# Zero products in the gaps of two attention chains, down blocks begun with the first weight chunk, half of one batch's attention moved under down products

## The chip, the cores and the metric

The kernel runs on one core of one Trainium2 chip. The metric is the time of one execution on the device in microseconds. A run of a kernel is one execution; a *round* runs the kernel before and the changed one on the same chip.

## The reference

```python
# q, k, v: (8, 8, 576, 64), phi: (8, 8, 576, 32)
a = exp(phi - max(phi, axis=2)); a = a / sum(a, axis=2)
k_m = einsum('bhsm,bhsd->bhmd', a, k)          # 32 memory slots a head
v_m = einsum('bhsm,bhsd->bhmd', a, v)
attn = softmax(q @ k_m^T / 8)                  # 576 x 32 a head
x = (attn @ v_m) transposed to (4608, 512)
out = ((x @ w_a) * (x @ w_b)) @ w_out          # 512 -> 1536 -> 512
```

## The kernel before

In what follows PE is the matrix engine (TensorE), ACT is ScalarE, DVE VectorE and POOL GpSimd; PSUM is the memory that PE's results go to. The kernel never forms x. It *folds* v_m into w_a and w_b for each batch (`vab`), so that an *up step* multiplies these with the normalised attention `A`: four matmuls for `pa`, four for `pb`, a cast of `pa` on ACT, a product on DVE that leaves 128 rows of the hidden layer in `ht`. *Down products* then multiply `ht` with `w_out`; twelve of them make one block of 128 tokens (`po`).

```python
def fold(lo, hi, z, ...):          # 8 small matmuls (64x32 tiles), then two casts
    pvas = [banks.tile([P, 512], F32, name="pva") for _ in range(2)]
    ...                            # pva[g] <- kvT, w_a or w_b columns lo:hi
    # vab[g] <- pva[g]: g = 0 on ACT, g = 1 on DVE

def up(b, i):
    for hf in range(2):
        pa = ps_up.tile([P, HALF], F32, name="pa")      # two buffers
        ...                                             # two matmuls, a_sb <- pa on ACT
    yield                                               # a place for something else
    for hf in range(2):
        pb = ps_up.tile([P, HALF], F32, name="pb")      # two buffers
        ...                                             # two matmuls, ht <- a_sb * pb on DVE
    yield
```

The kernel divides PSUM into eight banks: two for `pa`, two for `pb`, and four that everything else takes in rotation, `banks`: sums, transposes, scores, denominators `pD`, normalisations `pR`, folds and the open block `po` of down products. The order of PE's work is written by hand (cuts are marked with dots):

```python
fill(28)                                  # zero products: keep PE busy while loads are on their way
run(0, "exp0 exp1 ks0 kt0")               # batch 0: exponentials, k sums, transposes
fill(2)
run(0, "qt0 qt1 ks1 kt1")
run(0, "sc0 qt2 qt3")                     # q transposes (DVE), scores
fill(4)
run(0, "sc1 vs vt dn vh0a nr0 nr1 nr2 nr3 vh0b")   # v sums, denominators, folds, normalisations
ups(steps(0, 0, 2), named(0, "- vh1a - vh1b"))     # up steps, with folds at places between them
ups(steps(0, 2, 4), named(0, "- va1a - va1b"))
load(2)
ups(steps(0, 4, 8), named(0, "- va2a - va2b"))
ups(steps(0, 8, 12), named(1, "exp0 exp1"))
run(1, "ks0 kt0 ks1 kt1 qt0 qt1 sc0 qt2 qt3")      # batch 1's chain
some(8)                                            # eight down products of batch 0
...
ups(steps(1, 6, 12), named(2, "qt0 exp0 qt1 exp1 - kv0 kv1 - kvt - qt2 sc0 qt3 sc1"), 0)
work.ready = 2 * S // P * NFF
for x in "va0a dn va0b va1a nr0 nr1 va1b nr2 va2a nr3 va2b".split():
    run(2, x)                                      # the stage of folds and products:
    work.advance(2)                                # two down products behind each item
```

From batch 2 on, every up step has down products beside it, at a rate that uses up what is ready.

The softmax here doesn't subtract the row's maximum and nothing guards it: scores larger than these inputs give would overflow.

## Time and profile before

| | before |
|---|---|
| median of 4 runs | 273.26 us (272.68 to 273.96) |
| span of the profiled run | 271.8 us |
| PE busy | 257.4 us, 95% of the span |
| last fold of batch 0 | at 30.27 us |
| first down product | at 42.33 us |
| batch 1's first pa | at 57.96 us |
| batch 2's first pa | at 86.02 us |
| batch 3's first pa | at 112.10 us |

The kernel is bound by PE from 90 us on, so the reader should look for holes before that. The last five rows of the table are landmarks: they are instructions that both kernels have, so the time between two of them can be compared stage by stage. Busy times of the stages, from the windows view (window, length, busy us and count of PE, PEld, DVE, ACT and POOL, granted clock, DMA share, GB/s):

```profile
30.27:57.96 27.69, 24.88 (x334) 12.43 (x333) 15.17 (x35) 10.49 (x25) 6.68 (x9) 0.94 1.20 228
57.96:77.00 19.04, 17.69 (x253) 10.58 (x251) 15.61 (x37) 12.80 (x33) 2.35 (x4) 1.00 1.05 219
77.00:86.02 9.02, 8.62 (x93) 3.12 (x87) 6.59 (x11) 4.53 (x9) 0.62 (x1) 1.00 0.90 162
86.02:112.10 26.08, 26.08 (x322) 14.68 (x321) 19.39 (x44) 15.30 (x39) 2.98 (x4) 1.00 0.63 123
112.10:271.80 159.70, 154.50 (x1565) 85.38 (x1557) 91.83 (x203) 79.95 (x197) 5.95 (x8) 1.00 0.36 77
```

The rows are: batch 1's chain and first down blocks; batch 1's ups; the stage of folds and products; batch 2's ups; the rest. In the first, PE has 2.8 us of holes, and a mean clock of 0.94 over 27.7 us hides 1.7 us more. In the second it has 1.4 us of holes, while its busy time is stretched by waits inside the matmul records. The third has 0.4 us of holes and the fourth none; the 5.2 us of the last lie behind the last matmul, which ends at 266.6 us.

### The profile page before, as it was taken

The numbers are of one execution on the slowest core, as the hardware profiler recorded it, in microseconds if no ns is written. First come the engines' busy times: TensorE is split into PE (matmuls) and PEld (weight loads), VectorE is DVE, ScalarE is ACT, GpSimd is POOL, SyncE is SP. The second block draws the span as 40 slices with busy tenths as digits, with TensorE's granted clock in tenths as the row PEclk, the third lists the DMA queues.
The fourth block names the chain that finished last, engine by engine and source line by source line (L and its number), as shares of the span: only waits on it lengthen the run. The fifth ranks groups of instructions, "written<-read, shape, count | busy, mean of one in ns | idle before, by whom it ended". The sixth has DMA issues, their size and how long they took to land.

```text
span 271.8 us, 7173 instructions
## 1 busy us (share of the span) xinstructions
PE 257.4 (95%) x2898; PEld 138.5 (51%) x2898; DVE 166.7 (61%) x366; ACT 135.3 (50%) x331; POOL 36.5 (13%) x59
## 2 busy tenths in 40 slices
PE   8869978999989999999999999999999999999992
PEld 3435552446624555555555555555555555666540
DVE  7456863459778568855885567855885477443200
ACT  3037742078555565645565465726563555544220
POOL 8943332010310310031001300000000000000000
PEclk9998997999999999999999999999999999999999
DMA  7999999999893597059615891111112111112243
GB/s 156 195 202 204 252 207 230 229 269 256 165 207 77 128 200 142 14 134 188 134 39 166 136 207 39 41 41 38 34 26 62 42 39 41 40 41 57 65 111 77
DMA packets 25858, 33.49 MB, mean 123 GB/s; under 512 B 1889, under 2 KB 20321, under 8 KB 25825
## 3 DMA queue, kind: packets, MB, share of 16 engines
q0 software_dynamic: 19536, 23.01, 47.2%
q1 hardware_dynamic: 6288, 10.03, 14.7%
q8 instruction: 22, 0.36, 0.5%
q14 instruction: 12, 0.09, 0.1%
HBM read 42.47 MB, written 9.44 MB: 191 GB/s over the span
## 4 chain that ended last, share of the span: by engine, by line
PE 92%; DVE 4%; issue 1%; ACT 1%; DVEq 0%; ACTq 0%
PE po L385 35%; PE pa L455 19%; PE pb L464 19%; PE pva L341 6%; PE pw L119 3%; PE pkv L216 3%; PE pscore L296 2%; DVE qT L203 2%; PE pR L327 1%; DVE ht L467 1%; PE pT L245 1%; PE pk L265 1%; PE pT L251 1%; PE pD L315 1%; PE pT L280 0%
## 5 line engine op out<-in xcount | busy, mean ns | idle before, releaser
L385 PE MATMUL po<-wo_sb,ht 128*128 128x512 f16 x432 | 121.0, 383 | 0.2 <-ACT E L305 0.2
L467 DVE TENSOR_TENSOR ht<-a_sb,pb 128x288 f16<-128x288 f16 x192 | 78.0, 446 | 35.2 <-PE pb L464 30.8
L458 ACT CAST a_sb<-pa 128x288 f16<-128x288 f32 x192 | 67.6, 407 | 34.2 <-PE pa L455 32.4
L464 PE MATMUL pb<-A,vab 128*128 128x288 f16 x384 | 64.8, 288 | 0.5
L455 PE MATMUL pa<-A,vab 128*128 128x288 f16 x384 | 64.0, 289 | 0.2 <-ACT a_sb L458 0.2
L385 PEld LDWEIGHTS <-ht 128*128 128x128 f16 x432 | 41.3, 98 | 24.6 <-issue 3.8
L351 ACT CAST vab<-pva 128x512 f16<-128x512 f32 (+1 forms) x54 | 29.5, 555 | 44.5 <-PE pva L341 44.4
L455 PEld LDWEIGHTS <-vab 128*128 128x128 f16 x384 | 33.0, 98 | 24.8 <-issue 11.3
L464 PEld LDWEIGHTS <-vab 128*128 128x128 f16 x384 | 35.5, 98 | 19.4 <-issue 1.9
L353 DVE CAST vab<-pva 128x512 f16<-128x512 f32 x46 | 31.6, 687 | 7.3 <-PE pva L341 6.7
L394 ACT ACTIVATE o_sb<-po 128x512 f32<-128x512 f32 (+1 forms) x36 | 21.6, 604 | 23.2 <-PE po L385 23.2
L305 ACT ACTIVATE E<-pscore,rphi 128x288 f16<-128x288 f32 x32 | 14.3, 497 | 26.5 <-PE pscore L296 26.5
L203 DVE STREAM_TRANSPOSE qT<-q_sb 128x576 f16<-128x576 f16 x32 | 24.1, 764 | 0.0
L330 DVE SCALAR_TENSOR_TENSOR A<-E,rphi,pR 128x288 f16<-128x288 f16 x32 | 15.9, 512 | 8.7 <-PE pR L327 8.7
L341 PEld LDWEIGHTS <-kvT 64*32 64x32 f16 x400 | 5.9, 89 | 19.3 <-issue 18.1
L78 POOL DMA_DIRECT2D phi_sb<-in_phi_dram x7 | 5.3, 755 | 68.3 <-ACT exp_sb L194 50.9
L319 DVE RECIPROCAL rD<-pD 128x144 f16<-128x144 f32 x8 | 8.5, 1057 | 7.8 <-PE pD L315 7.8
L231 DVE CAST kvm<-pkv 128x128 f16<-128x128 f32 (+1 forms) x16 | 4.1, 267 | 13.8 <-PE pkv L216 13.8
L194 ACT ACTIVATE exp_sb<-phi_sb 128x576 f16<-128x576 f32 x16 | 10.9, 695 | 2.6 <-DMA phi_sb<-in_phi_dram 2.6
L119 PE MATMUL pw<-warm 128*128 128x512 f16 x34 | 9.9, 450 | 1.3 <-DVE warm L113 1.3
L341 PE MATMUL pva<-wa_sb,kvT 64*32 64x512 f16 (+1 forms) x200 | 10.3, 378 | 0.5 <-DVE kvT L253 0.4
L296 PE MATMUL pscore<-qT,kvT 32*32 32x288 f16 x256 | 8.0, 295 | 2.7 <-DVE qT L203 2.7
(44 smaller groups left out, 109.6 us busy)
## 6 DMA issues: line engine op xcount, KB each, us to landing
out_dram<-o_sb SPq DMA_DIRECT2D x72, 128.0 KB, 2.4
kv_sb<-in_v_dram POOLq DMA_DIRECT2D x8, 576.0 KB, 9.9
phi_sb<-in_phi_dram POOLq DMA_DIRECT2D x7, 576.0 KB, 5.2
kv_sb<-in_k_dram POOLq DMA_DIRECT2D x7, 576.0 KB, 7.7
q_sb<-in_q_dram POOLq DMA_DIRECT2D x6, 576.0 KB, 9.3
wo_sb<-in_moe_w_out_dram POOLq DMA_DIRECT2D x3, 512.0 KB, 17.2
q_sb<-in_q_dram POOLq DMA_DIRECT2D x4, 288.0 KB, 12.7
wa_sb<-in_moe_w_a_dram POOLq DMA_DIRECT2D x2, 512.0 KB, 13.3
```

Source lines behind the costliest of these rows:

```text
L119: nc.tensor.matmul(pw[:, :cols], warm[:, :P], warm[:, :cols], start=True, stop=True)
L203: nc.vector.transpose(out=t["qT"][:, hp, :], in_=qs[b][:, hp, :])
L330: nc.vector.scalar_tensor_tensor(out=attn[b][:, g, sl], in0=t["E"][:, g, sl], scalar=t["rphi"][:, g:g + 1], in1=pR, op0=ALU.mult, op1=ALU. ...
L341: nc.tensor.matmul(pvas[g][32 * j:32 * j + 32, 0:hi - lo], t["kvT"][64 * r:64 * r + 64, 4 + g, M * j:M * j + M], w_sbs[z][64 * r:64 * r + ...
L351: nc.scalar.copy(out=vabs[b][z][:, g, lo:hi], in_=pvas[g][:, 0:hi - lo])
L353: nc.vector.tensor_copy(out=vabs[b][z][:, g, lo:hi], in_=pvas[g][:, 0:hi - lo])
L385: nc.tensor.matmul(po, hts[pair][:, i, P * c:P * (c + 1)], wo_sb[:, i, :], start=(i == 0), stop=(i == NFF - 1))
L394: nc.scalar.mul(out=o_sb[:, :cut], in_=po[:, :cut], mul=1.0 / (CS * CS))
L455: nc.tensor.matmul(pa, vab[0][:, g, fs], A[:, g, HALF * hf:HALF * (hf + 1)], start=(g == 0), stop=(g == 1))
L458: nc.scalar.copy(out=a_sb, in_=pa)
L464: nc.tensor.matmul(pb, vab[1][:, g, fs], A[:, g, HALF * hf:HALF * (hf + 1)], start=(g == 0), stop=(g == 1))
L467: nc.vector.tensor_tensor(out=ht[:, i, t0:t0 + HALF], in0=a_sbs[hf], in1=pb, op=ALU.mult)
```

## The change

Its intent, in four parts, A to D:

- **A**, the first chain: 28 zero products in front become 16, and others fill the gaps behind each short group, so that PE's clock holds.
- **B**: for batches 0 and 1, `pb` of the odd steps takes one of the four rotating banks.
- **C**, the second chain: k sums of batch 1 go among the last up steps of batch 0, and down products begin in front of the first scores instead of behind them, about when the first third of `w_out` lands.
- **D**: two q transposes and both scores of batch 2 leave batch 1's ups for the stage of folds and products, which grows from 11 to 17 places.

```diff
--- before.py
+++ after.py
@@ -459,7 +459,7 @@
             a_sbs.append(a_sb)
         yield
         for hf in range(2):
-            pb = ps_up.tile([P, HALF], F32, name="pb")
+            pb = banks.tile([P, HALF], F32, "pb") if b < 2 and i % 2 else ps_up.tile([P, HALF], F32, name="pb")
             for g in range(2):
                 nc.tensor.matmul(pb, vab[1][:, g, fs], A[:, g, HALF * hf:HALF * (hf + 1)],
                                  start=(g == 0), stop=(g == 1))
@@ -490,43 +490,56 @@
         for f in named(b, names):
             f()
 
-    fill(28)
-    run(0, "exp0 exp1 ks0 kt0")
-    fill(2)
-    run(0, "qt0 qt1 ks1 kt1")
-    run(0, "sc0 qt2 qt3")
-    fill(4)
-    run(0, "sc1 vs vt dn vh0a nr0 nr1 nr2 nr3 vh0b")
+    fill(16)
+    run(0, "exp0 exp1 ks0")
+    fill(3, 256)
+    run(0, "kt0 qt0 qt1")
+    fill(7)
+    run(0, "sc0 ks1")
+    fill(3, 256)
+    run(0, "kt1 qt2 qt3")
+    fill(5)
+    run(0, "sc1")
+    fill(3)
+    run(0, "vs dn vt")
+    fill(3, 256)
+    run(0, "nr0 nr1 vh0a nr2 nr3 vh0b")
+    fill(4, 256)
     ups(steps(0, 0, 2), named(0, "- vh1a - vh1b"))
     ups(steps(0, 2, 4), named(0, "- va1a - va1b"))
     load(2)
     ups(steps(0, 4, 8), named(0, "- va2a - va2b"))
-    ups(steps(0, 8, 12), named(1, "exp0 exp1"))
+    ups(steps(0, 8, 12), named(1, "exp0 exp1 - - - ks0 kt0 ks1"))
     early = early_downs()
 
     def some(n):
         for _ in range(n):
             next(early, None)
 
-    run(1, "ks0 kt0 ks1 kt1 qt0 qt1 sc0 qt2 qt3")
+    run(1, "kt1 qt0 qt1")
+    fill(4)
+    some(8)
+    run(1, "sc0 qt2 qt3")
     some(8)
     run(1, "sc1")
     some(8)
     run(1, "dn")
     some(8)
     run(1, "nr0 nr1 nr2 nr3")
-    some(10)
+    some(8)
     run(1, "vs")
     some(4)
-    run(1, "vt va0a")
+    run(1, "vt")
+    some(2)
+    run(1, "va0a")
     some(2)
     run(1, "va0b")
     some(99)
     load(3)
     ups(steps(1, 0, 6), named(1, "- va1a - va1b - va2a - va2b"), 0)
-    ups(steps(1, 6, 12), named(2, "qt0 exp0 qt1 exp1 - kv0 kv1 - kvt - qt2 sc0 qt3 sc1"), 0)
+    ups(steps(1, 6, 12), named(2, "- exp0 qt0 exp1 qt1 - kv0 - kv1 - kvt"), 0)
     work.ready = 2 * S // P * NFF
-    for x in "va0a dn va0b va1a nr0 nr1 va1b nr2 va2a nr3 va2b".split():
+    for x in "qt2 sc0 qt3 sc1 va0a va0b dn va1a va1b nr0 va2a nr1 va2b nr2 - nr3 -".split():
         run(2, x)
         work.advance(2)
     every = "qt0 exp0 qt1 exp1 qt2 kv0 kv1 - kvt sc0 qt3 sc1 - va0a dn va0b nr0 va1a nr1 va1b nr2 va2a nr3 va2b"
```

## The prediction

> **What bounds the kernel now.** I read the page's slices first, then two-microsecond windows of the first 100 us, then the timeline there, and last the landing time of each transfer. The slices:
>
> ```profile
> PE   8869978999989999999999999999999999999992
> PEclk9998997999999999999999999999999999999999
> DMA  7999999999893597059615891111112111112243
> ```
>
> From slice 13 on (about 90 us) PE has no holes until the drain of the last products. The matmul time of that part stays the same in the changed kernel, so all that can be won lies before 90 us: in PE's holes and in slices at a lower clock. The windows show two places:
>
> ```profile
> 18.00:20.00 2.00, 1.29 (x17) 0.94 (x11) 1.55 (x3) 0.65 (x2) 1.00 (x2) 0.77 1.35 204
> 20.00:22.00 2.00, 1.94 (x14) 1.01 (x13) 1.09 (x3) 1.16 (x4) 0.71 (x1) 0.50 1.24 207
> ...
> 38.00:40.00 2.00, 1.34 (x77) 0.88 (x68) 1.22 (x6) 0.00 (x0) 0.74 (x1) 1.00 1.24 207
> 40.00:42.00 2.00, 0.55 (x18) 0.17 (x19) 1.72 (x4) 0.00 (x0) 0.75 (x1) 1.00 1.24 206
> 42.00:44.00 2.00, 2.00 (x20) 0.83 (x20) 1.23 (x2) 0.89 (x2) 0.74 (x1) 0.75 1.24 209
> 44.00:46.00 2.00, 2.00 (x21) 0.42 (x19) 0.00 (x0) 0.04 (x1) 0.00 (x0) 0.50 1.22 207
> 46.00:48.00 2.00, 2.00 (x12) 0.70 (x14) 0.00 (x0) 0.85 (x2) 0.00 (x0) 0.90 1.14 322
> ```
>
> The columns are window, length, busy time of PE, PEld, DVE, ACT, POOL, then the clock, the DMA share and GB/s. PE is busy 1.89 of 4 us in 38 to 42 (batch 1's attention chain), and right after that the clock is halved; the same follows the thin stretch 16 to 20 of batch 0's chain. The last two columns matter as much: DMA runs at some 207 GB/s without a break. It is a bound of its own up to 82 us, and once PE already waits for it:
>
> ```profile
> 30.26 0.11 PEld L341 LDWEIGHTS <-kvT 64*32 64x32 f16 x8 [0.26 <-DMA wb_sb<-in_moe_w_b_dram]
> ```
>
> That is the last fold of batch 0, which needs the last quarter block of w_b, issued at 14.80 with 15.4 us to landing, so in place at 30.2. The third stretch is batch 1's up step, 58 to 77.65:
>
> ```profile
> 58.00:64.65 6.65, 6.65 (x73) 3.91 (x72) 5.52 (x12) 5.52 (x14) 0.00 (x0) 1.00 1.16 271
> ...
> 66.90:77.65 10.75, 9.16 (x175) 5.29 (x173) 8.25 (x22) 6.17 (x17) 2.97 (x4) 1.00 0.96 180
> 77.65:86.18 8.53, 8.37 (x80) 3.05 (x80) 6.61 (x11) 4.13 (x8) 0.00 (x0) 1.00 0.86 155
> ```
>
> Here no products stand beside the ups, and DVE paces PE: in 60 to 70 it is busy 9.48 of 10 us.
>
> **What the Trainium skill says.** "TensorE: Matmul & The Clock Gate", Part 1 (The HAM clock gate): the clock is halved after an idle window of about 3.4 us and comes back after a busy one; K is binary. The trace agrees: time at half speed is 2 x (1 - clock) x 2 us a window, 1.0 + 2.0 + 0.4 = 3.4 us for the second dip; the first adds up to 3.4 as well (0.77, 0.50, 0.87). The trace adds that PE need not be quite idle: 47% busy was enough, 69% (12 to 14) was not. Same page, Part 2 (Step-by-step): matmuls stay in program order, only weight loads are pulled ahead; so a fold that waits for weights holds up everything behind it, as at 30.26. "Perfetto Trace Analysis", Roofline: 16 DMA engines move about 435 GB/s for one core. These transfers cast float32 to float16, so 207 GB/s written is 414 read: the queue is full, and no landing time of the weights can move forward.
>
> **The change part by part.** Durations are those of before at full clock: one product 0.22 us (8 in 1.83), one up step 0.98 (8 matmuls; pa 0.49 and pb 0.49 in the chain), one fold 0.34, one half of the k sums 0.64, scores 0.4 a half, pR 0.5, v sums 0.7.
>
> *Batch 0's chain with fills.* The first fill falls from 28 to 16 products, so ks0 can start at k's landing (1.31 + 5.8 = 7.1) instead of 9.53, and the clock should hold. The chain itself still needs v (landed at 14.6) and rD (1.06) and four normalisations (2 us), so I put the first up step at about 19 instead of 20.64, and steps 0 and 1 save perhaps 1.4 us of half clock. Some 3 us early: but the folds stand at fixed places, and their weights land at 22.6, 25.2, 27.7 and 30.2, while before runs those folds at 25.48, 26.90, 28.82 and 30.26. The lead over the weights shrinks to nothing at the last. So PE waits at each of these folds instead, and stands at 30.26 just where it stood: gain 0.
>
> *30.26 to the end of batch 1's k sums.* Steps 6 to 11 took 7.1 us against 5.9 of matmul time. pb in a second set of buffers removes the waits for DVE (0.1 a step), but the exponentials (1.27 us on ACT) still hold up a_sb and with it pa of step 10. ks0, kt0 and ks1 now lie among the last steps. I work it out to ks1 ending at 38.7 instead of 39.6.
>
> *Down blocks early.* kt1 follows at 39.4 to 39.6 (its cast waits for DVE), four fills 0.87 end at 40.5; the first chunk of w_out is there at 22.93 + 17.2 = 40.1, the second at 42.6, the third at 45.2, v at 48.1. Then PE is full: 48 products (10.6), two scores 0.8, pD 0.25, pR 0.5, v sums 0.7, transposes 0.25, two folds 0.7 = 13.8, so the ups of batch 1 start at about 54.4 instead of 57.96. This holds the clock dip (3.4 us at half clock, 1.7 lost) and the holes of 38 to 42.3, less the fills. The products that used to cover the casts of the last fold are used up by now, so the first pb waits about half a microsecond: I count a gain of 3.5 less 0.3, 3.2.
>
> *Batch 1's ups without half of batch 2's attention.* Before: 57.96 to 77.0, 19.0 us. The first six steps are bound by DVE (0.82 of ht and 0.68 of vab a step with a fold) and stay near 7.9. Steps 6 to 11 lose two transposes (1.54 of DVE) and two scores: DVE 6 x 0.82 + 1.54 + 0.88 + 0.56 = 7.9, PE 5.88 + 1.0 + 0.6 = 7.5, so about 8.4 instead of 11.1. Sum 16.3 plus 0.3 of waiting: 16.6. That is 2.4 earlier, of which 0.8 is only matmul time moved: gain 1.6 to 1.7 (PE's lead is now about 5).
>
> *The stage of folds and products.* Before 9.2 us against 8.1 of matmuls. After: 17 places with 34 products (7.5) + six folds 2.0 + pD 0.25 + pR 0.5 + scores 0.8 = 11.1, and I leave the loss to bank waits at 1.0: three banks remain beside the held one in both. Gain 0; the ten further products are taken from the next stage.
>
> *Batch 2's ups.* 36 products before, 26 after. Matmul time there falls by 2.2 to 24.0 us, while DVE keeps its 20. In the second half a step has one fold and one normalisation on DVE: 0.82 + 0.69 + 0.51 = 2.0, against PE's 2.2 less 0.18 = 2.0. DVE becomes level with PE: I take off 0.6.
>
> Sum: 3.2 + 1.65 + 0 - 0.6 = 4.3 us, and 0.4 for bank waits that the spacing of the 17 places may save: 4.7. 273.6 - 4.7 = 268.9.
>
> **The rivals.** *First: the whole of the early gain comes through.* If the folds of batch 0 didn't wait for weights, the 3 us of the first chain would come on top: 265.9. Against it stand the DMA columns at their ceiling and the wait at 30.26. *Second: the holes move.* If the first products wait for the w_out chunk or the first fold steps of batch 1 are held by ACT (four o_sb of 0.55 beside vab and a_sb), some 1.5 us go: 270.5. For it: DMA is full, and w_out's margin by my working is 0.4 us. *Third: DVE eats the moved work.* If DVE, at 83% in batch 2's ups before, paces both halves of that stage with 10 products fewer, it costs up to 2.2 and leaves 270.5 as well. *Fourth: bank shortage.* pb of the odd steps shares four banks with the folds and held sums; a pb that waits for a fold's eviction would bring back 0.5 to 1 us. Against it: banks are taken in rotation. None of these makes the kernel slower than before, as the fills fall from 34 full ones to 35 full and 13 half ones, all in holes but four.
>
> **Range and chances.** Each of the three main terms (3.2, 1.65, 0.6) is good to about 1 us, together about 1.8; the range is 266.6 to 271.2. The limit of 2% is 268.2, a gain of 5.5, a little past my middle: 0.36 for faster, 0.62 for the same, 0.02 for slower.
>
> **What would show it.** Right: clock 1.00 in 18 to 24 and in 42 to 48; new waits of PE for wa_sb and wb_sb at the folds between 22 and 30, with the last of them still at 30.2; the first product at about 40.5, batch 1's first pa at about 54.4; batch 2's ups at about 83, with DVE over 85% busy in them. The early part is wrong if the last fold of batch 0 runs well before 30 (the transfers were not the bound), the middle if the first product comes after 41, the last if PE shows holes or longer steps after 83.

## More of the kernel before

A program on one core has no second die to compare with, so small differences are compared only where the kernels share a chip and the runs of the kernel before.

## The result, and the profile after

The changed kernel took 270.36 us (median of 4 runs, 269.79 to 270.95), the kernel before 273.26 in the same rounds. The ratio is 0.9893 with a 95% interval of 0.9858 to 0.9927: faster by about 1%, the same by the measure of 2%. Ratios here are the mean time of one kernel's runs over that of the other's of the same rounds, so they are not quite the ratio of the medians quoted beside them.

The slices of the page of the changed kernel:

```profile
PE   8979989999999999999999999999999999999992
PEclk9998999999999999999999999999999999999999
DMA  7999999999993595169515971111111111112243
```

(9 stands for 90% or more of a fortieth of the span, on PEclk for the granted clock.) The dip of the clock near 44 us is gone, one near 20 us is still there, and DMA is saturated as long as before. The windows of the second chain, changed kernel:

```profile
38.00:40.00 2.00, 1.67 (x50) 0.94 (x48) 1.37 (x5) 0.70 (x2) 0.74 (x1) 1.00 1.24 208
40.00:42.00 2.00, 2.00 (x17) 0.94 (x18) 1.67 (x5) 0.00 (x0) 0.75 (x1) 1.00 1.25 207
42.00:44.00 2.00, 2.00 (x25) 0.76 (x24) 1.30 (x2) 0.60 (x2) 0.55 (x1) 1.00 1.24 208
44.00:46.00 2.00, 2.00 (x25) 0.75 (x24) 0.00 (x0) 0.69 (x2) 0.19 (x1) 1.00 1.23 211
```

PE is busy 3.67 of 4 us from 38 to 42, where it was busy 1.89 in the kernel before, and the clock stays at 1.00. The last fold of batch 0 in the timeline of the changed kernel (start, length, what it is; in brackets the idle time before it and what ended that):

```profile
30.75 0.11 PEld L341 LDWEIGHTS <-kvT 64*32 64x32 f16 x8 [0.37 <-DMA wb_sb<-in_moe_w_b_dram]
```

It still waits for the last part of `w_b`, and as that part landed half a microsecond later in this profile, it also runs half a microsecond later than before. The stages of the changed kernel, the same rows as shown of before:

```profile
30.75:55.26 24.51, 23.66 (x336) 12.18 (x337) 14.23 (x34) 10.00 (x24) 6.68 (x9) 1.00 1.21 220
55.26:71.70 16.44, 16.28 (x229) 10.28 (x221) 14.15 (x34) 12.29 (x32) 2.23 (x3) 1.00 1.13 264
71.70:85.48 13.78, 13.21 (x132) 4.63 (x130) 9.53 (x17) 6.33 (x12) 0.74 (x1) 1.00 0.87 156
85.48:108.98 23.50, 23.50 (x310) 13.51 (x309) 18.57 (x43) 14.46 (x37) 2.98 (x4) 1.00 0.68 132
108.98:268.70 159.72, 154.50 (x1565) 85.37 (x1557) 91.82 (x203) 79.95 (x197) 5.95 (x8) 1.00 0.36 77
```

| stage | before | predicted | after |
|---|---|---|---|
| to the last fold of batch 0 | 30.27 | 30.26 | 30.75 |
| to batch 1's first pa | 27.69 | 24.1 | 24.51 |
| batch 1's ups | 19.04 | 16.6 | 16.44 |
| folds and products | 9.02 | 12.1 | 13.78 |
| batch 2's ups | 26.08 | 24.6 | 23.50 |
| the rest | 159.70 | unchanged | 159.72 |

The second column is read off the steps of the prediction (54.4 - 30.26, 71.0 - 54.4 and so on). The rest is the same to 0.02 us, so the whole of the difference lies in five numbers. Two of them are off the prediction by more than a microsecond: the stage of folds and products (1.7 too long) and batch 2's ups (1.1 shorter than forecast). With the half microsecond by which the last fold was late, 0.4 in the second row, 0.2 the other way in the third, and the credit of 0.4 that the prediction had added for bank waits, the forecast gain of 4.7 becomes 4.7 - 1.7 + 1.1 - 0.5 - 0.4 + 0.2 - 0.4 = 3.0, the profile's 3.1 but for rounding.

One figure serves all that follows: **from the last fold to the end**, 241.50 us before and 237.91 after (worked out from the times in the traces themselves, as the pages print the end to 0.1 us only). The time up to the last fold changes from execution to execution with the transfers and the clock; the time from it on hardly does in the changed kernel. In c0 it had its last fold at 31.27 and needed 237.90 from there, and e1, e5 and e6, which change only what lies in front, needed 237.90 to 237.91. For the kernel before there is one trace, and its 241.50 contain a dip of the clock.

### The profile page after: what moved, and what is told of

The parts are those of the page before. It is cut to its first block, busy times and chain, and to the rows that moved or that the text cites. A ratio compares the mean times of both kernels' runs of the same rounds, so it can differ in the third digit from the quotient of the medians.

```text
span 268.7 us, 7200 instructions
## 1 busy us (share of the span) xinstructions
PE 258.4 (96%) x2912; PEld 138.9 (52%) x2912; DVE 166.4 (62%) x366; ACT 135.4 (50%) x331; POOL 36.5 (14%) x59
## 4 chain that ended last, share of the span: by engine, by line
PE 84%; DMA 10%; DVE 2%; issue 1%; POOL 1%; ACT 1%; ACTq 0%; DVEq 0%; POOLq 0%
PE po L385 34%; PE pa L455 19%; PE pb L464 17%; DMA wb_sb<-in_moe_w_b_dram 6%; PE pva L341 6%; DMA kv_sb<-in_v_dram 4%; PE pkv L216 2%; PE pscore L296 2%; PE pR L327 1%; PE pT L245 1%; PE pD L315 1%; PE pT L251 1%; POOL q_sb L90 1%; DVE qT L203 1%; DVE ht L467 0%
## 5 line engine op out<-in xcount | busy, mean ns | idle before, releaser
L464 PE MATMUL pb<-A,vab 128*128 128x288 f16 x384 | 63.8, 288 | 0.3
L119 PE MATMUL pw<-warm 128*128 128x512 f16 (+1 forms) x48 | 13.4, 415 | 1.3 <-DVE warm L113 1.3
L341 PE MATMUL pva<-wb_sb,kvT 64*32 64x512 f16 (+1 forms) x200 | 10.6, 382 | 0.1
```

The costliest lines, as they stand in the source:

```text
L341: nc.tensor.matmul(pvas[g][32 * j:32 * j + 32, 0:hi - lo], t["kvT"][64 * r:64 * r + 64, 4 + g, M * j:M * j + M], w_sbs[z][64 * r:64 * r + ...
L464: nc.tensor.matmul(pb, vab[1][:, g, fs], A[:, g, HALF * hf:HALF * (hf + 1)], start=(g == 0), stop=(g == 1))
```

## The experiments

The theory after reading the two traces: (1) the last fold is tied to its transfer, so part A is worth little as long as the transfer is there; (2) part C carries the gain; (3) part D wins in batch 1's ups, and loses it in the stage of folds and products, where a fold must wait for the banks of its predecessors; the prediction's term for that stage was too small by 1.7 us. Rivals are in the expectations. Each kernel was run 6 times, on three chips; medians of the kernel before were 273.83 (e1 to e4), 274.72 (c0, e5 to e7) and 274.06 (e8 to e11).

### The changed kernel again (c0)

> The changed kernel itself, as the measure for the runs beside it. Expected 270.2 to 270.7 us, with the last fold of batch 0 at the landing of the last part of w_b (30.5 to 31.3) wherever the clock held in the first chain, and no more than 0.5 us spread between runs with and without a dip.

Measured: 270.90 us (269.8 to 272.0), ratio 0.9884 [0.9833, 0.9935]. In this profile the clock held through the first chain, and the timeline shows what the theory says is hidden there:

```profile
28.72 0.41 PE L341 MATMUL pva<-wa_sb,kvT 64*32 64x512 f16 x8 [0.65 <-DMA wa_sb<-in_moe_w_a_dram]
...
31.27 0.41 PE L341 MATMUL pva<-wb_sb,kvT 64*32 64x512 f16 x8 [1.06 <-DMA wb_sb<-in_moe_w_b_dram]
```

With the clock at 1.00, PE reaches the last two folds 0.65 and 1.06 us before their weights. The first chain is faster, and the transfer takes the gain back. The expected time (270.2 to 270.7) was missed by 0.2, and so was the expected spread: five runs at a mean clock of 0.994 to 0.997 took 269.8 to 271.2, and one at 0.982 took 272.0.

### The first chain of before in the changed kernel (e1)

```diff
-    fill(16)
-    run(0, "exp0 exp1 ks0")
-    fill(3, 256)
 ...
-    run(0, "nr0 nr1 vh0a nr2 nr3 vh0b")
-    fill(4, 256)
+    fill(28)
+    run(0, "exp0 exp1 ks0 kt0")
+    fill(2)
+    run(0, "qt0 qt1 ks1 kt1")
+    run(0, "sc0 qt2 qt3")
+    fill(4)
+    run(0, "sc1 vs vt dn vh0a nr0 nr1 nr2 nr3 vh0b")
```

> The changed kernel with the first chain of before (28 fills in front, no fills in the small gaps, old order). Theory (the last fold of batch 0 waits for the last part of w_b, which lands at about 30.5 us whatever PE does before): the last fold stays at 30.2 to 30.8 and the time within 0.4 us of the changed kernel's 270.4, although a clock dip of 3.4 us near 20 us should be back. Rival (the fills of the first chain carry part of the gain): the last fold at 31.5 or later and 1 us or more is lost, 271.4 or more.

Measured: 270.87 us (270.26 to 271.95), ratio 0.9881 [0.9837, 0.9925]. From the last fold to the end 237.90, so nothing behind it changed. In the profile the last fold ran at 31.92, a miss for both sides: the dip lasted two windows in place of one (clock 0.50 from 20 to 24 us, 0.65 and 0.64 on either side of that). Runs with a mean clock of 0.992 and 0.994 took 270.67 and 270.26, those at 0.984 to 0.989 took 270.5 to 271.95. Against e2, which has the new chain and is otherwise equal from the last fold on, the median is 0.5 us higher. So part A is worth about half a microsecond by these medians, though the ranges of the runs overlap. That it comes through the clock is likely: between 16 and 28 us the four profiles of the old chain have one dip (before) or two in a row (e1, e6, e8), the ten of the new chain one (six of them) or none (c0, e3, e4, e7).

### The last third of w_b not transferred, with both chains (e5, e6)

The fold reads the middle third of `w_b` a second time. The results are wrong.

```diff
-    load_wab(1024, 1536)
+    nc.gpsimd.dma_start(out=wa_sb[:, :, 1024:1536], in_=wa_rows[:, :, 1024:1536])
 ...
-                        w_sbs[z][64 * r:64 * r + 64, hp, lo:hi],
+                        w_sbs[z][64 * r:64 * r + 64, hp, (lo - 512 if z and lo == 1024 else lo):(hi - 512 if z and lo == 1024 else hi)],
```

> The changed kernel without the transfer of the last third of w_b (0.5 MB); the fold reads the middle third again, so the result is wrong on purpose. Theory (transfers pace batch 0's ups once the clock holds): the wait of about 1 us at the last fold is gone, it runs at 29.8 to 30.3, and the time falls by 0.7 to 1.2 us against the changed kernel of the same rounds. Rival (the wait hides another limit, such as the casts on ACT and VectorE): under 0.3 us.

> The same without the last third of w_b, and with the first chain of before; wrong on purpose too. Theory (the old chain with its dips gets to the last fold just when its weights land, so it cannot use the free transfer): within 0.4 us of the old chain with the transfer (about 0.4 above the changed kernel), and 1.0 to 1.6 us above the new chain without the transfer: that is what the fills would be worth if the weights were there. Rival (the first chain is worth nothing at all): no difference between the two chains here either.

Measured: e5 (new chain) 269.92 us (269.56 to 270.46), e6 (old chain) 271.03 us (269.7 to 271.78); the changed kernel 270.90. Without the transfer the new chain gains 1.0 us, and its last fold runs at 29.87 even with a dip in the profile. The old chain stays at 271.03, with the last fold at 31.42, and gains nothing. The two chains differ by 1.1 us here and by about 0.5 with the transfer. That is the theory's first point: by the medians the fills are worth about a microsecond, and the transfer of `w_b` hides half of it.

### Part C alone in the kernel before (e8)

```diff
-    ups(steps(0, 8, 12), named(1, "exp0 exp1"))
+    ups(steps(0, 8, 12), named(1, "exp0 exp1 - - - ks0 kt0 ks1"))
 ...
-    run(1, "ks0 kt0 ks1 kt1 qt0 qt1 sc0 qt2 qt3")
+    run(1, "kt1 qt0 qt1")
+    fill(4)
+    some(8)
+    run(1, "sc0 qt2 qt3")
 ...
-    some(10)
+    some(8)
 ...
-    run(1, "vt va0a")
+    run(1, "vt")
+    some(2)
+    run(1, "va0a")
```

> The kernel before with the second chain of the change alone (k sums of batch 1 among the last ups, down blocks begun with the first chunk): old first chain, no extra buffers for pb, no move of batch 2's attention. Theory (this part carries nearly all of the gain): from the last fold of batch 0 to the end 238.2 to 238.8 us instead of 241.5, and 2.5 to 3.5 us under the kernel before of the same rounds. Rival (the parts only work together): under 1.5 us.

Measured: 272.58 us (271.0 to 273.58), the kernel before 274.06; ratio 0.9944 [0.9902, 0.9986]. From the last fold to the end 238.88, just outside the expected range: 2.6 of the 3.6 us. The whole time fell by only 1.5, which is the rival's number (under 1.5); the interval of the ratio stands for a gain of 0.4 to 2.7 us, so it does not exclude 2.6. In the profile the last fold ran at 32.03, behind a clock of 0.50 from 20 to 26 us. But the kernel before has the same first chain, and none of its runs in this call has a trace: why the whole gained less than the stage is not shown, and neither is that part C needs part A.

e2 below has parts A, B and C, and 237.95 from the last fold on; A changes nothing there (e1). So B, the extra buffers for `pb`, is worth 238.88 - 237.95 = 0.9 us there.

### Batch 2's attention placed as before (e2)

```diff
-    ups(steps(1, 6, 12), named(2, "- exp0 qt0 exp1 qt1 - kv0 - kv1 - kvt"), 0)
+    ups(steps(1, 6, 12), named(2, "qt0 exp0 qt1 exp1 - kv0 kv1 - kvt - qt2 sc0 qt3 sc1"), 0)
 ...
-    for x in "qt2 sc0 qt3 sc1 va0a va0b dn va1a va1b nr0 va2a nr1 va2b nr2 - nr3 -".split():
+    for x in "va0a dn va0b va1a nr0 nr1 va1b nr2 va2a nr3 va2b".split():
```

> The changed kernel with batch 2's attention placed as before (all of it under batch 1's ups, 12 places with products). Theory (the stage of folds and products lost to waits for banks and for VectorE most of what the shorter ups won): batch 1's ups last 18.8 to 19.1 us, the stage 9.0, batch 2's ups 26.1, and the time is 0.2 to 0.6 us above the changed kernel. Rival (the move is worth the 1 us net of the prediction, or more): 1.0 us or more above it.

Measured: 270.37 us (269.58 to 270.84), ratio 0.9854 [0.9807, 0.9900]. From the last fold to the end 237.95, against 237.91 of the changed kernel: **part D as written is worth 0.04 us.** The theory's direction holds, though it expected 0.2 to 0.6; the 1 us net of the prediction does not. By stages: batch 1's ups 18.65 (a little under what was expected), the stage 9.02, batch 2's ups 26.08.

### The places of the stage in another order (e3)

```diff
-    for x in "qt2 sc0 qt3 sc1 va0a va0b dn va1a va1b nr0 va2a nr1 va2b nr2 - nr3 -".split():
+    for x in "qt2 sc0 qt3 - sc1 va0a dn va0b - nr0 va1a nr1 va1b nr2 va2a nr3 va2b".split():
```

> The changed kernel with the same 17 places of the fold stage in another order: the scores apart by three places, no two folds next to one another where it can be had, the reciprocal of the denominators before the second fold. Theory (folds wait for the banks of the fold before, and one waits for the 1.06 us reciprocal in VectorE's queue): the stage shrinks from 13.8 to 12.2 to 12.8 us and the time falls by 1.0 to 1.5 us to 269.0 to 269.4. Rival (the stage is long because of PE's own cost for switching between products and small tiles, which stays): the stage stays within 0.4 us of 13.8.

Measured: 269.50 us (269.12 to 270.04), ratio 0.9827 [0.9786, 0.9869]; from the last fold to the end 237.09, which is 0.8 less than the changed kernel. The time is 0.1 above the theory's range, and the stage took 12.99 us (72.20 to 85.19), 0.2 longer than expected. One wait of 0.31 us for the reciprocal's bank was still there, now in front of `va0b`. So the order was part of the loss and not all of it.

### Folds of the stage in banks of their own (e7)

No up step runs in that stage, so the four banks of `pa` and `pb` lie idle. This run gives them to the folds and leaves the order alone.

```diff
-            pvas = [banks.tile([P, 512], F32, name="pva") for _ in range(2)]
+            pvas = [ps_up.tile([P, 512], F32, name="pva", tag="pa" if z == 0 else "pb") if b == 2
+                    else banks.tile([P, 512], F32, name="pva") for _ in range(2)]
```

> The changed kernel, order of places unchanged, with batch 2's folds written to the four banks of the ups, which are idle in that stage, in place of the four that scores, denominators, normalisations and the open product block share. Theory (bank waits and the place behind the reciprocal are what the stage lost, about 1.7 us beyond the prediction): the stage falls from 13.8 to 12.2 to 12.7 us and the time by 1.1 to 1.5 us. Rival (the reciprocal and the casts in VectorE's queue are the limit, whichever bank they read): less than 0.5 us.

Measured: 269.00 us (268.63 to 269.46), the changed kernel 270.90; ratio to before 0.9817 [0.9774, 0.9860]. The medians are 1.9 us apart; the profile gives 236.35 from the last fold on, 1.6 less. The stage, in the windows of e7:

```profile
71.93:84.16 12.23, 12.14 (x133) 4.29 (x130) 9.36 (x17) 6.32 (x12) 0.74 (x1) 1.00 0.97 172
```

It fell from 13.78 to 12.23 us. That this is next to the 12.1 of the prediction is chance, as the section on the prediction shows. What went away is best seen at the third fold. In the changed kernel's timeline:

```profile
77.33 1.06 DVE L319 RECIPROCAL rD<-pD 128x144 f16<-128x144 f32 x1
...
77.75 0.39 PE L341 MATMUL pva<-wa_sb,kvT 64*32 64x512 f16 x1
78.44 0.41 PE L341 MATMUL pva<-wa_sb,kvT 64*32 64x512 f16 x7 [0.31 <-DVE rD L319]
```

and in that of e7:

```profile
77.12 0.60 PE L386 MATMUL po<-wo_sb,ht 128*128 128x512 f16 x2
77.65 0.41 PE L342 MATMUL pva<-wa_sb,kvT 64*32 64x512 f16 x8
```

A fold takes two banks. In the changed kernel the first matmul of `va1a` found its bank free at 77.75. The second needed the bank in which `pD` lay, and the reciprocal read that until 78.39. PE keeps the program's order, so the other seven matmuls and all products behind them waited. In e7 the eight start together, although the reciprocal stands where it stood and DVE's queue is the same. That rules out the rival.

### As before in the placing, and folds in banks of their own (e11)

> The changed kernel with batch 2's attention placed as before, and with its folds in the idle banks of the ups. Theory (the move is worth 1.0 to 1.4 us, which bank waits of the longer stage took back): from the last fold to the end 237.5 to 238.0, so 1.2 to 1.6 us more than the changed kernel with folds in those banks (236.3). Rival (the free banks help both placements alike, the move itself is worth nothing): 236.3 to 236.7.

The edit is that of e2 and that of e7 together. Measured: 269.71 us (269.0 to 270.26); from the last fold to the end 237.24. It lies between theory and rival. The free banks help this order too, by 237.95 - 237.24 = 0.7 us, and the moved order by 1.6. With banks to spare, part D is worth 237.24 - 236.35 = 0.9 us, near the 1.05 that the prediction has for it (1.65 less 0.6). So the bank waits did take back what D had won, but the theory overstated by how much the old order was free of them.

### No fills before the first down block (e4)

```diff
     run(1, "kt1 qt0 qt1")
-    fill(4)
     some(8)
```

> The changed kernel without the four zero products in front of the first down block. Theory (the first chunk of w_out is there at 40.4, so the fills delay the first product from 40.5 to 41.1): the first product at 40.4 to 40.6 and 0.5 to 0.7 us less, 269.8. Rival (the chunk or the transposes of q hold the next step anyway, or the clock falls without them): no change, or a dip to half clock near 42 and 1 us more.

Measured: 270.10 us (269.46 to 270.35); from the last fold to the end 237.21, 0.7 less than with the fills; all six runs have a clock of 0.996 to 1.000. The first product came at 40.91, later than expected only because the last fold was at 31.26: between the two lie 9.65 us, against 10.36 with the fills. The fills guarded against a dip that does not come.

### All of it together (e9, e10)

```diff
-    ups(steps(0, 4, 8), named(0, "- va2a - va2b"))
-    ups(steps(0, 8, 12), named(1, "exp0 exp1 - - - ks0 kt0 ks1"))
+    ups(steps(0, 4, 8), named(0, "- va2a - - - va2b"))
+    ups(steps(0, 8, 12), named(1, "exp0 - exp1 - - ks0 kt0 ks1"))
```

with the edits of e7 and e4; e10 has in addition

```diff
-    for x in "qt2 sc0 qt3 sc1 va0a va0b dn va1a va1b nr0 va2a nr1 va2b nr2 - nr3 -".split():
+    for x in "qt2 sc0 qt3 - sc1 va0a va0b dn va1a va1b nr0 va2a nr1 va2b nr2 nr3 -".split():
```

> The changed kernel with batch 2's folds in the idle banks of the ups, without the four fills before the down blocks, the last fold of batch 0 one step later, and the two exponentials of batch 1 one place apart. Theory (the four act in different stages and add up: 1.6, 0.7, up to 0.9, up to 0.4): 267.0 to 267.8 us, clear of 2% under the kernel before.

> The one before it, and in the fold stage a place without work put between the third transposition of q and the second scores, taken from the end of the list. Theory (the second scores wait 0.38 us for banks that the exponentials of the first still read): 0.3 to 0.4 us less than without it. Rival (the next fold then waits instead): no difference.

Measured: e9 269.37 us (267.67 to 270.7), a miss: it was to be under 267.8. e10 267.95 us (267.73 to 269.75), ratio 0.9788 [0.9753, 0.9823]: the fastest of all, 2.1% under the kernel before by the ratio, though the interval reaches across the 2% line. From the first down product to the end e9 takes 226.00 us and e10 225.62: the 0.38 us that the place between the scores was to bring. The other microsecond between the two medians is not explained by the edit. The profile of e9 shows where it can come from:

```profile
40.94 1.90 PE L386 MATMUL po<-wo_sb,ht 128*128 128x512 f16 x8 [1.62 <-DMA wo_sb<-in_moe_w_out_dram]
```

PE is now early enough to stand 1.62 us before the first down product, waiting for the first third of `w_out`; in the profile of e10 that wait is 0.47 us. The transfers have become the bound of the first 41 us, and whether they come late differs from one execution to the next. That all of e9's slow runs (270.1 to 270.7) are such cases is likely, and not shown, as only one run has a trace.

## Why the prediction was right or wrong

**The time** was inside the range: 270.36 for 268.9 (266.6 to 271.2), and the most likely class, within 2%, came out. The gain was 2.9 us in the medians and 3.1 in the profiles where 4.7 was forecast. Step by step:

- *Batch 0's chain, "gain 0"*: the mechanism was right. The last fold was at the landing of `w_b` in the profiles of the changed kernel, and e5 shows 1.0 us that only this transfer hides. Details were wrong. The waits foretold for each of these folds came at the last one alone (0.37 us; in c0 at the last two), and the fills do not fall: by the prediction's own count they rise, from 34 full ones to 35 full and 13 half. The first up step was put at about 19 and ran at 21.20, later than before, so the "some 3 us early" never existed: the v sums stood still for about 1 us in both kernels (see the end), the dip remained in this profile, and four more fills were in front of the up step. And the landing was not fixed to 0.1 us: it was 0.5 later here. By the medians the chain still gave half a microsecond, most likely through the clock.
- *Batch 1's chain and the down blocks, 3.2*: right. The stage shrank by 27.69 - 24.51 = 3.2 us, the first product came at 41.11 for a forecast 40.5, and the second dip went. (By the prediction's own sign, a first product after 41, this step would count as wrong; but the last fold was 0.5 late.) e8 gives 2.6 of the total to part C. The size missed by 0.4: the stage was to shrink by 3.5, to 24.1, and the 3.2 are what was left after 0.3 for a wait in the next one.
- *Batch 1's ups, 16.6*: 16.44. Right. Of the 2.6, e2 has 0.4 without the move (19.04 to 18.65) and the move brings the other 2.2. The 0.4 are a net: with part C alone (e8) the stage took 19.47, and `pb`'s buffers bring 0.8 of it.
- *The stage, "I leave the loss to bank waits at 1.0 ... Gain 0"*: **this step failed.** The forecast stage of 12.1 us took 13.78. The working had three banks for both orders and took the loss of the old order for the new one; the further credit of 0.4 "for bank waits that the spacing of the 17 places may save" had the wrong sign. But the new order puts folds in pairs, `va0a va0b dn va1a va1b`, so that a fold comes on banks that the one before has just filled, and on `pD`. e7 measures the term: 1.55 us in the stage, 1.6 in the whole. With its own banks the stage takes 12.23. e10 takes out another 0.38, the second scores' wait for banks, so bank waits cost 1.9 us where the working had 1.0 for all losses. Of the 2.7 us between the working's 11.1 and 13.78 some 0.8 are left after both. By an estimate they are a cost that the working did not have: in e7 two products take 0.52 to 0.54 us in front of each of the nine groups of small tiles, in place of 0.44 (see the end), which makes about 0.8.
- *Batch 2's ups, 24.6 with 0.6 taken off for DVE*: 23.50, so 1.1 better, for two reasons. The working had ten products fewer in that stage, and there are twelve (60 ready, less 22 before and 34 after): at 0.216 us that is 2.6, exactly 26.08 - 23.50. And DVE took nothing: PE was busy all the time and DVE 18.57 of 23.50, 79%, where over 85% was expected. Steps with a fold took 1.98 us from pa to pa, the forecast 2.0, so DVE kept level without ever stopping PE. By luck this made up for two thirds of the failed step.

Of the rivals, the first (the early gain comes through) was wrong and the second (first products wait for `w_out`) appeared only in e9 and e10, with other fills gone. The third (DVE paces batch 2's ups) did not come. The second and the third had 270.5, next to the measured 270.36, and neither for what in fact happened. The fourth, bank shortage, was named for `pb` and dismissed with "banks are taken in rotation"; it came true for folds, and rotation is what hands a fold the bank of a slow reader.

What stays open: why transfers land up to 1 us apart between executions of the same kernel, and why the clock dips for one window or for two.

## What to carry to other kernels

Before counting a gain on an early stage, write the landing times of its inputs beside the times at which they are used: a stage that is early against its transfers waits for them at its last consumer, whatever was saved before. When work moves into a stage, count who holds each PSUM bank and for how long, not only how many banks there are; idle banks of a neighbouring stage were worth more here (1.6 us, two lines) than the move they made room for (0.9 us). And read a change from a fixed instruction to the end, so that the scatter of the beginning does not cover a tenth of a per cent behind it.

## What the Trainium skill lacked or had wrong

- "TensorE: Matmul & The Clock Gate", Part 1 and Why this matters for your kernels: the page asks for no gap of more than about 3 us. Shorter gaps were enough here: in the kernel before the clock was 0.50 from 42.99 to 46.40 us, after 3.41 us in which PE was busy 48% and its longest single gap was about 1.1 us. It also fell after 3.41 us with PE busy 61% (changed kernel, 15.88 to 19.29) and 72% (e5, 15.06 to 18.47), while 3.41 us at 49% in e9 (38.90 to 42.31) were followed by the full clock. So PE's busy share alone does not foretell it, and the prediction's pair of 47% and 69% is no rule. The page calls the phase free-running and puts the cost of the ramp at under 1% of a typical span; here executions of the same kernel before within one call had mean clocks of 0.975 to 0.991 and took 275.6 to 272.4 us, a spread as large as the effect of the change. The length of a dip agrees with the page: 3.4 us, or two of them in a row (e8: 0.50 from 20 to 26). A run's mean clock is worth listing beside its time.
- "TensorEngine Tiling (Array Packing)", Key Properties, says that changing the tiling mode drains the engine and gives no figure. In e7 two products took 0.54 us where a fold or the denominators followed (76.34 to 76.88) and 0.44 where a matmul on the full array followed (78.87 to 79.31): about 0.1 us a change, an estimate. The prediction's 0.22 a product, from runs of eight, left this out.
- No page that was read says, in transfers or in time, how far GpSimd can run ahead of the transfers that it issues. In the changed kernel some 17 us of transfers were in its queue, and each of the nine issues from 14.49 to 30.99 us waited for the landing of an earlier transfer: the last part of `w_b` was issued at 14.49 us, when v landed, and each of the three chunks of `w_out` took 17.0 us from issue to landing.
- "Runtime: NRT & Kernel Launch", Instruction fetch mechanics, says that crossing a block of the instruction buffer is mostly hidden. In the v sums of batch 0 PE stood still without a wait that the profile knows, always after its 223rd matmul. The kernel before, with 34 fills in front, and e1, also with 34:

```profile
15.02 0.72 PE L216 MATMUL pkv<-kv_sb,exp_sb 64*32 64x64 f16 x69
16.73 0.21 PE L216 MATMUL pkv<-kv_sb,exp_sb 64*32 64x64 f16 x3 [0.98 <-issue]
```

```profile
17.30 0.21 PE L216 MATMUL pkv<-kv_sb,exp_sb 64*32 64x64 f16 x3 [1.68 <-issue]
```

The changed kernel, with 37 fills, splits the same 72 matmuls 66 to 6, three earlier, and stands for 1.04 us. That the place follows the count of instructions speaks for an instruction fetch behind saturated transfers; no run took it apart, and where PE waited 0.80 to 1.04 us for v in front of the sums (e3, e4, e9) the gap is not there.
